# The second MLP's first 256 rows, summed on TensorE from x2 and the last expert's kept tiles

## The chip, the cores and the metric

The kernel runs on one core of a Trainium2 chip. The metric is the device time of one execution in microseconds, the median of several runs; lower is better. The profile's engines are PE (TensorE matmul), PEld (TensorE weight load), DVE (VectorE), ACT (ScalarE), POOL (GpSimd) and SP (SyncE, which here issues most of the DMAs).

## The reference

Three stages follow each other. An attention with gates and a running state gives 3072 tokens of 320 features. A mixture of 8 experts sends each token to the one expert that its gate logits choose; the expert's row is scaled by a gate weight and lands in the token's row of the result. A second MLP of width 2048 runs over all 3072 rows. Cut to what matters here:

```python
x = attn_out.transpose(0, 2, 1, 3).reshape(B * S, H * D)     # 3072 x 320
e_idx = np.argmax(x @ w_gate, axis=1)
out = np.zeros((N, D))
for e in range(8):
    mask = e_idx == e
    h = np.maximum(x[mask] @ w1[e], 0.0)                      # 320 -> 1024
    out[mask] = gate_w[mask, None] * eom[mask, e, None] * (h @ w2[e])
h = out @ w_in                                                # 320 -> 2048
return np.maximum(0.01 * h, h) @ w_out
```

## The kernel before, in words

Attention sorts the tokens on the fly into slots by expert. In the expert loop, each expert takes 3 or 4 tiles of 112 or 128 tokens: GpSimd gathers the tokens by indirect DMA, TensorE computes the first half for all of them (`ph`) and then, tile by tile, the second half (`po`, 24 matmuls a tile). ScalarE reads each `po` tile out of PSUM with the token's gate as scale (`yo`), and GpSimd scatters the rows by indirect DMA to their places in the DRAM tensor `x2` (`put`, printed in the profile as `x<-yo,ms`). The last expert has 3 tiles of 112 tokens. Between two scatters GpSimd writes a one-element `gap`; the scatters are declared independent of each other.

While an expert runs, the weights of the next but one are loaded and split into a high and a low part (`w1h`, `w1l`, `w2h`, `w2l`). In the last expert these are the second MLP's weights, loaded by SP as `r<-wf_in` and `r<-wf_out`.

Experts that got more tokens than their tiles hold are served by a loop of `overflow_tile` (`tc.For_i`, line 1351). With these inputs it makes no trip, but each engine goes through its branch. Then the second MLP runs over `GROUPS` of rows: 256, then five groups of 512, then 256. A group's rows are loaded from `x2` (`x2r`), turned so that features lie on partitions (`pxm` by TensorE for the first group, `xtm` by VectorE for the others), and split (`xhm`, `xlm`); 16 blocks `p` of 8 matmuls each follow, whose results ScalarE, VectorE and GpSimd turn into `lk`, `g2h` and `g2l`; then the second half (`po`) and the store.

Around the change these lines set the order; the two `keep_warm` calls are matmuls whose result nobody reads (12 ahead of the loop, 7 behind it):

```python
keep_warm(nc, psum, wts[E].w1h[:, 0], WARM[1])
...
    with tc.For_i(0, more, 1) as r:
...
xrs = {0: rows(0)}
ctx.enter_context(tc.manual_schedule(engines=ORDERED))
keep_warm(nc, psum, wts[E].w1h[:, 0], WARM[2])
for f in range(4):
    wts[E + 1].split2(f, V)
x = Tokens(nc, ap, psum, ident, xrs.pop(0), "m0").all()
```

Under `manual_schedule` the four compute engines keep the order in which the code is written. Outside of it (from the end of the expert block to the second `manual_schedule`) a scheduler may move instructions; in the order before, three of the four `w2h` casts and one `w2l` of `split2` stand ahead of the loop. A DMA waits on semaphores on the engine that issues it. DMAs take eight semaphore lanes in turn, `DMAHW0` to `DMAHW7` for those of SP and ScalarE, `DMASW0` to `DMASW7` for GpSimd's.

Of the kernel before, what the change touches and what calls it, by code (L numbers as in the profile page):

```python
# [10 lines left out]
F32 = mybir.dt.float32  # L11
# [5 lines left out]
ALU = mybir.AluOpType  # L17
# [500 lines left out]
class Router:  # L518
# [51 lines left out]
        nc.gpsimd.iota(self.meta, pattern=[[P, NC_], [S, B], [0, 4]], base=0, channel_multiplier=1)  # L570
        self.order.setup()

    def clear(self):

        put = self.nc.sync.dma_start
        late = lambda b: self.xd[b * S + (NC_ - 2) * P : (b + 1) * S].rearrange("(t p) e -> p t e", p=P)
        return [lambda: put(self.slots.rearrange("(p r) w -> p r w", p=P), self.init)] + [
            lambda b=b: put(late(b), self.zero[:, None, :].to_broadcast([P, 2, DM])) for b in range(B)
        ]

    def sink(self, c, b):
        if b == 0:
# [343 lines left out]
class Tokens:  # L926
# [8 lines left out]
    def dup(self):  # L935
        self.nc.vector.tensor_copy(self.xr[:, :, DM:DW], self.xr[:, :, 2 * P : DM])
# [72 lines left out]
class Expert:  # L1009
# [39 lines left out]
    def out(self, w, gs, ms, j, tag):  # L1049
        self.put(self.rows(w, gs, ms, j, tag), ms, j)  # L1050

    def rows(self, w, gs, ms, j, tag):
# [3 lines left out]
        mm2(self.nc, po, gs, ws, j)  # L1056
        return self.scaled(po, ms, j, tag)

    def scaled(self, po, ms, j, tag):
        yo = (self.ypool or self.pool).tile([P, DM], F32, tag="yo", name=f"yo{tag}_{j}", bufs=2 if self.ypool else 3)  # L1060
        yo = yo[: ms.shape[0]]
        self.nc.scalar.activation(yo, po, AF.Copy, scale=ms[:, j, 2:3].bitcast(F32))
        return yo

    def put(self, yo, ms, j):
        if self.puts is not None:
            self.nc.gpsimd.memset(self.gap, 0)
        put = self.nc.gpsimd.indirect_dma_start(
            out=self.x2,
            out_offset=bass.IndirectOffsetOnAxis(ap=ms[:, j, 1:2], axis=0),  # L1070
            in_=yo,
            in_offset=None,
            bounds_check=NT - 1,
            oob_is_err=False,
        )
        if self.puts is not None:
            apart(self.tc, put, self.puts, "every token is in one slot")


class Fill:  # L1080
# [65 lines left out]
def mlstm_moe_mlp(  # L1146
# [37 lines left out]
    def slots_of(e):  # L1184
        return ms[: ROWS[e], e, 0 if e else NJ // 2 : TILES[e]]
# [12 lines left out]
    with ExitStack() as actx:  # L1198
        h0 = actx.enter_context(tc.tile_pool(name="h0pool", bufs=1))
        exh = Expert(nc, h0, psum, ident, xd, x2, True, cpool)  # L1200
        exh.tc, exh.puts, exh.gap = tc, [], cpool.tile([1, 1], I32, name="gap2")
        msa = ms[:, 0, 0 : NJ // 2]
        fill = Fill(exh, msa, wts[0])

        def bumped():
            load_slots(0, 0, NJ // 2, P)

        router = Router(tc, actx, psum, ident, w_gate, w_og, slots, xd, stage, order, bumped)
        half = {}
# [12 lines left out]
        parts = w.steps([V, V, G, V, V, V, G])  # L1222
        todo = []

        def clear():
            todo.extend(router.clear())
# [10 lines left out]
        feed.update({i: [nxt] for i in (4, 5, 6, 7, 8, 9, 12, 13, 14, 15)})  # L1237
# [5 lines left out]
    wslot.append(ctx.enter_context(tc.tile_pool(name="wslot1", bufs=1)))  # L1243
    with ExitStack() as mctx:
        mp = mctx.enter_context(tc.tile_pool(name="mpool", bufs=2))
        cv = mctx.enter_context(tc.tile_pool(name="cvpool", bufs=1))
# [18 lines left out]
        for e in range(E):  # L1265
# [72 lines left out]
            if tk:  # L1338
                tk.turn()
                xs = tk.split()  # L1340
                tk = ex.x(ex.gather(slots_of(e + 2), e + 2), e + 2) if e + 2 < E else None
            for j in range(nj):
                ex.out(wts[e], gs, m, j, e)
                for act in late[j]:
                    act()

    keep_warm(nc, psum, wts[E].w1h[:, 0], WARM[1])
    with ExitStack() as octx:
        op = octx.enter_context(tc.tile_pool(name="opool", bufs=1))
        ex = Expert(nc, op, psum, ident, xd, x2, True)  # L1350
        with tc.For_i(0, more, 1) as r:
            e = nc.values_load(order.owner[0:1, ds(r, 1)], engines=SP, min_val=0, max_val=E - 1)
            row = nc.values_load(order.rows[0:1, ds(r, 1)], engines=SP, min_val=0, max_val=E * REG - P)
            overflow_tile(nc, op, ex, slots, w1, w2, e, row)

    ap = ctx.enter_context(tc.tile_pool(name="ap", bufs=2))
    gp = ctx.enter_context(tc.tile_pool(name="gp", bufs=1))
    GROUPS = [(0, HCAP)] + [(r, CAP) for r in range(HCAP, NT - CAP, CAP)] + [(NT - HCAP, HCAP)]

    def rows(i):  # L1360
        r, n = GROUPS[i]
        t = ap.tile([P, NJ * DM], F32, tag="x2r", name=f"x2r{i}", bufs=1)
        w = DM if i else DW
        t = t[:, : n // P * w].rearrange("p (j w) -> p j w", w=w)
        for j in range(n // P):
            nc.sync.dma_start(t[:, j, 0:DM], x2[r + j * P : r + (j + 1) * P])
        return t

    xrs = {0: rows(0)}
    ctx.enter_context(tc.manual_schedule(engines=ORDERED))  # L1370
    keep_warm(nc, psum, wts[E].w1h[:, 0], WARM[2])
    for f in range(4):
        wts[E + 1].split2(f, V)
    x = Tokens(nc, ap, psum, ident, xrs.pop(0), "m0").all()
    ws = [(wts[E + f // 8].w2h[:, f % 8], wts[E + f // 8].w2l[:, f % 8]) for f in range(F2 // P)]
    for i, (r, n) in enumerate(GROUPS):
        nxt, turns = None, []
        if i + 1 < len(GROUPS):
            nxt = Tokens(nc, ap, psum, ident, rows(i + 1), f"m{i + 1}")
            turns = nxt.pieces()  # L1380
        gs, lks = [], []

        def parts():
# [87 lines left out]
```

## Time and profile before

| | |
|---|---|
| median of 3 runs | 755.69 us (753.97 to 757.65) |
| the profiled execution | 753.32 us, its span 751.6 us |
| TensorE busy | 716.1 us, 95% of the span |
| VectorE, ScalarE, GpSimd busy | 449.8, 356.3, 350.2 us |
| mean granted TensorE clock | 0.979 of full |

Times in the rows are microseconds from the span's start. L1351 is line 1351 of the kernel before. A row of a timeline has start, duration, engine, line, operation, output from inputs, the shape and the count of instructions merged in it; in brackets stands the idle time ahead of it and what ended it. A row of the table by stages has the stage, its length, then for PE, PEld, DVE, ACT and POOL the busy time and the number of instructions, then the granted clock, the mean busy share of the 16 DMA engines and the GB/s. `SPq` and `PEldq` are the instruction queues (sequencers) of SP and TensorE, which carry semaphore waits, branches and the issue of DMAs.

### The profile page before, as it was taken

What the parts mean: (1) busy time and instruction counts of PE and PEld (TensorE: products, weight loads), DVE (VectorE), ACT (ScalarE), POOL (GpSimd) and SP (SyncE); (2) the same over time, 40 slices, a digit from 0 to 9 for tenths busy, and PEclk for the clock granted to TensorE, in tenths of its full rate; (3) what the DMA queues carried; (4) which work ended last, traced back from release to release, by engine and by line L of the source; (5) the groups of instructions that cost most, each with busy time, mean ns of one, the idle gap of its engine ahead of it and who ended that gap; (6) DMA issues with size and microseconds to landing.
All of it is one profiled execution on the core that took longest, in us unless ns stands there. A gap on an engine that the chain in (4) does not pass through costs nothing. (4 is left out here: it accounts for less than half of the span.)

```text
span 751.6 us, 14585 instructions
## 1 busy us (share of the span) xinstructions
PE 716.1 (95%) x5450; PEld 667.9 (89%) x5450; DVE 449.8 (60%) x936; ACT 356.3 (47%) x803; POOL 350.2 (47%) x396
## 2 busy tenths in 40 slices
PE   8798998899799999999998999999999999999998
PEld 6798987888689899999997989988988988988998
DVE  8988889674556758797765757048048048037020
ACT  5678677532463644663455355055045045046041
POOL 8758688655235474635123355046046046037041
PEclk9998999999799999999999999999999999999999
DMA  5887787411877677756662011001001000000000
GB/s 170 240 245 201 212 214 193 106 55 29 292 232 239 231 274 224 260 202 215 180 201 61 11 44 37 27 9 36 27 10 36 28 10 18 27 10 0 27 11 17
DMA packets 61743, 87.51 MB, mean 116 GB/s; under 512 B 8318, under 2 KB 53385, under 8 KB 60392
## 3 DMA queue, kind: packets, MB, share of 16 engines
q1 hardware_dynamic: 55880, 67.43, 30.0%
q10 hardware_dynamic: 2336, 10.75, 4.2%
q0 software_dynamic: 3456, 8.39, 3.5%
q8 instruction: 43, 0.70, 0.4%
q14 instruction: 28, 0.23, 0.1%
HBM read 67.69 MB, written 19.33 MB: 116 GB/s over the span
## 5 line engine op out<-in xcount | busy, mean ns | idle before, releaser
L1388 POOL TENSOR_TENSOR g2l<-lk,g2h 128x512 fp32r<-128x512 f32 (+1 forms) x112 | 126.6, 1133 | 214.0 <-ACT g2h L1387 203.7
L1397 DVE TENSOR_TENSOR lk<-p,lk 128x512 f32<-128x512 f32 (+1 forms) x112 | 68.9, 615 | 181.0 <-ACT lk L1396 179.1
L995 PE MATMUL p<-xhm,w1h 128*128 128x512 f32 (+1 forms) x336 | 119.6, 360 | 0.0
L995 PE MATMUL p<-xhm,w1l 128*128 128x512 f32 (+1 forms) x336 | 119.2, 359 | 0.0
L1006 PE MATMUL po<-w2h,g2l 128*128 128x320 f32 x384 | 118.7, 309 | 0.0
L1005 PE MATMUL po<-w2l,g2h 128*128 128x320 f32 x384 | 118.7, 309 | 0.0
L1004 PE MATMUL po<-w2h,g2h 128*128 128x320 f32 x384 | 118.6, 309 | 0.0
L1396 ACT ACTIVATE lk<-p 128x512 f32<-128x512 f32 (+1 forms) x112 | 60.1, 536 | 73.6 <-PE p L995 73.6
L995 PE MATMUL p<-xlm,w1h 128*128 128x512 f32 (+1 forms) x224 | 80.6, 360 | 0.0
L1004 PEld LDWEIGHTS po<-w2h,g2h 128*128 128x128 f32 x384 | 72.1, 188 | 0.2
L1005 PEld LDWEIGHTS po<-w2l,g2h 128*128 128x128 f32 x384 | 72.1, 188 | 0.2
L1411 ACT COPY yo<-po 128x320 f32<-128x320 f32 x24 | 10.2, 426 | 130.7 <-PE po L1006 130.7
L1006 PEld LDWEIGHTS po<-w2h,g2l 128*128 128x128 f32 x384 | 72.1, 188 | 0.0
L995 PEld LDWEIGHTS p<-xhm,w1l 128*128 128x128 f32 x336 | 63.5, 189 | 9.4
L995 PEld LDWEIGHTS p<-xhm,w1h 128*128 128x128 f32 x336 | 63.6, 189 | 9.4 <-DVE xhm L975 0.2
L1004 PE MATMUL po<-w2h,gh 128*128 128x320 f32 (+1 forms) x208 | 65.7, 316 | 0.0
L1005 PE MATMUL po<-w2l,gh 128*128 128x320 f32 (+1 forms) x208 | 65.0, 312 | 0.0
L1006 PE MATMUL po<-w2h,gl 128*128 128x320 f32 (+1 forms) x208 | 64.9, 312 | 0.0
L1387 ACT CAST g2h<-lk 128x512 fp32r<-128x512 f32 (+1 forms) x112 | 61.6, 550 | 1.6 <-DVE lk L1397 1.6
L957 DVE STREAM_TRANSPOSE xtm<-x2r 32x384 f32<-32x384 f32 (+3 forms) x144 | 59.6, 414 | 2.8
L995 PE MATMUL ph<-xh,w1h 128*128 128x384 f32 (+3 forms) x168 | 59.4, 354 | 0.0
L995 PE MATMUL ph<-xh,w1l 128*128 128x384 f32 (+3 forms) x168 | 59.3, 353 | 0.0
(252 smaller groups left out, 1547.9 us busy)
## 6 DMA issues: line engine op xcount, KB each, us to landing
r<-in_moe_w_dram SPq DMA_DIRECT2D x6, 1280.0 KB
r<-in_moe_w_dram SPq DMA_DIRECT2D x7, 1024.0 KB
raw<-in_moe_w_out_dram ACTq DMA_DIRECT2D x5, 1024.0 KB
r<-in_moe_w_dram SPq DMA_DIRECT2D x16, 256.0 KB
raw<-in_moe_w_in_dram ACTq DMA_DIRECT2D x4, 1024.0 KB
v<-in_v_dram SPq DMA_DIRECT2D x24, 164.0 KB
o<-in_o_gate_dram SPq DMA_DIRECT2D x6, 640.0 KB
k<-in_k_dram SPq DMA_DIRECT2D x24, 160.0 KB
```

What stands on the lines that cost most here:

```text
L957: self.nc.vector.transpose(out=xt[f, k].rearrange("p k (j t) -> p k j t", t=P)[:, :, :, t], in_=blocks[t, :, g].rearrange("p j k f -> p k ...
L995: nc.tensor.matmul(ps, a, b, start=(i == 0), stop=(i == len(seq) - 1))
L1004: nc.tensor.matmul(ps, gh[:, js], wh, start=(f == 0), stop=False)
L1005: nc.tensor.matmul(ps, gh[:, js], wl, start=False, stop=False)
L1006: nc.tensor.matmul(ps, gl[:, js], wh, start=False, stop=(f == n - 1))
L1387: nc.scalar.copy(gh, lk)
L1388: nc.gpsimd.tensor_sub(gl, lk, gh.bitcast(F32))
L1396: nc.scalar.activation(lk, pf, AF.Copy, scale=0.01)
L1397: nc.vector.tensor_max(lk, pf, lk)
L1411: nc.scalar.copy(yo, po[:, :DM])
```

## The change

A new class `Head` holds what the first 256 rows of the second MLP (`HCAP`) need, ahead of the loop.

- While the last expert runs, GpSimd writes the numbers 0 to 255 into `head_ids`; VectorE copies the token numbers of the expert's last two tiles and compares them, which gives two placing matrices `head_at` (112 x 256, a 1 where the slot's token is the row).
- Behind the first tile's scatter SP loads `x2[0:256]` into `head_x`. The last two tiles are read from PSUM into tiles of their own (`head_y`, `head_last`) and also scattered to `x2` as before.
- Behind the loop TensorE adds up, in PSUM and already turned, `head_x` (as plain matmuls against the identity) and the two kept tiles (each against its placing matrix). This takes the place of loading 256 rows from `x2` and transposing them.
- As `head_x` is read before the last two tiles are scattered, these 256 rows of `x2` are now cleared by a DMA of zeros in attention.
- The warm-up matmuls ahead of the loop go from 12 to 2, the 7 behind it go. The second `manual_schedule` begins right behind the loop, so all of `split2` stays behind it, and behind the split of the first rows. The next group's four loads are issued ahead of that split.

```diff
-WARM = (11, 12, 7)
+WARM = (11, 2)
...
-    def clear(self):
+    def clear(self, head):
...
+        ] + [lambda: put(head, self.zero[:, None, :].to_broadcast([P, 2, DM]))]
...
+    def keep(self, po, ms, j, yo, last):
+        g = ms[:, j, 2:3].bitcast(F32)
+        n = DM - 2 * P
+        self.nc.scalar.activation(yo, po, AF.Copy, scale=g)
+        both = po[:, None, 2 * P : DM].to_broadcast([po.shape[0], 2, n])
+        self.nc.scalar.activation(last.rearrange("p (c f) -> p c f", f=n), both, AF.Copy, scale=g)
...
+class Head:
...
+    def places(self, ms):
+        v, self.r = self.nc.vector, ms.shape[0]
+        v.tensor_copy(self.tok[: self.r], ms[:, 1:3, 1])
+        for j in range(2):
+            v.tensor_scalar(self.at[: self.r, j], self.ids[: self.r], self.tok[: self.r, j : j + 1], None, ALU.is_equal)
+
+    def load(self):
+        for j in range(HCAP // P):
+            self.nc.sync.dma_start(self.xr[:, j, 0:DM], self.x2[j * P : (j + 1) * P])
...
+    def turn(self, psum):
+        pts, mm, r = [], self.nc.tensor.matmul, self.r
+        for kt in range(3):
+            f = slice(kt * P, (kt + 1) * P)
+            pt = psum.tile([P, 512], F32, tag="ps", name=f"pxm0_{kt}")[:, :HCAP]
+            mm(pt, self.part(0, kt), self.at[:r, 0], start=True, stop=False)
+            for h in range(HCAP // P):
+                mm(pt[:, h * P : (h + 1) * P], self.xr[:, h, f], self.ident, start=False, stop=False)
+            pts.append(pt)
+        for kt, pt in enumerate(pts):
+            mm(pt, self.part(1, kt), self.at[:r, 1], start=False, stop=True)
+        return pts
...
+            if e == E - 1:
+                head.number(cv)
+                head.places(m)
             for j in range(nj):
-                ex.out(wts[e], gs, m, j, e)
+                if e == E - 1 and j:
+                    yo = head.yo[j - 1][: m.shape[0]]
+                    ex.rows(wts[e], gs, m, j, e, (yo, head.last[: m.shape[0], j - 1]))
+                    ex.put(yo, m, j)
+                else:
+                    ex.out(wts[e], gs, m, j, e)
+                    if e == E - 1:
+                        head.load()
...
+    ctx.enter_context(tc.manual_schedule(engines=ORDERED))
+    head.dup()
+    pts = head.turn(psum)
+    hctx.close()
...
-    xrs = {0: rows(0)}
-    ctx.enter_context(tc.manual_schedule(engines=ORDERED))
-    keep_warm(nc, psum, wts[E].w1h[:, 0], WARM[2])
+    nxt = Tokens(nc, ap, psum, ident, rows(1), "m1")
+    x = Tokens(nc, ap, psum, ident, head.xr, "m0")
+    x.pts = pts
+    x = x.split()
     for f in range(4):
         wts[E + 1].split2(f, V)
-    x = Tokens(nc, ap, psum, ident, xrs.pop(0), "m0").all()
```

GpSimd, the last expert's three scatters to `x2` (printed `x_79`), before. In brackets stands what the instruction waits for; a scatter waits for the earlier use of its own lane, so these three are on DMASW5, 6 and 7, and `L1351` is the loop's branch:

```order
L1068 DMA x_79<-yo_0_5408,ms 3072x320 [waits DMASW5_49,Activation_49]
L1067 MEMSET gap_91 1x1 [waits Pool_49]
L1068 DMA x_79<-yo_1_5443,ms 3072x320 [waits DMASW6_49,Activation_49]
L1067 MEMSET gap_91 1x1 [waits Pool_49]
L1068 DMA x_79<-yo_2_5476,ms 3072x320 [waits DMASW7_49,Activation_49]
L1351 COMPARE_AND_BRANCH
```

The same place in the changed kernel, where lines carry later numbers:

```order
L1106 IOTA head_ids 128x256
L1079 MEMSET gap_91 1x1 [waits Pool_49]
L1080 DMA x_79<-yo_0_5423,ms 3072x320 [waits DMASW5_49,Activation_49]
L1079 MEMSET gap_91 1x1 [waits Pool_49]
L1080 DMA x_79<-head_y_5392,ms 3072x320 [waits DMAHW3_49,DMAHW4_49,DMASW6_49,Activation_49]
L1079 MEMSET gap_91 1x1 [waits Pool_49]
L1080 DMA x_79<-head_y_5393,ms 3072x320 [waits DMASW7_49,Activation_49]
L1429 COMPARE_AND_BRANCH
```

The second scatter has gained two waits, for the lanes DMAHW3 and DMAHW4, and an `iota` stands ahead of the first.

SP in the changed kernel, from the last weights' loads to the loop's branch. ScalarE's casts wait for lanes 7, 0 and 1 for the three loads from `wf_in`, so the load from `wf_out` has lane 2 and the two of the head lanes 3 and 4:

```order
L803 DMA r_5326<-wf_in 128x2x1024 [waits DMAHW3_49,DMAHW2_49,DMAHW4_49,DVE_49,Activation_49]
L804 DMA r_5326<-wf_in 64x1024
L805 DMA r_5326<-wf_in 64x1024 [waits DMAHW1_49]
L811 DMA r_5389<-wf_out 128x8x320 [waits DMAHW5_49,DMAHW6_49,DVE_49,Activation_49]
L1119 DMA head_x<-x_79 128x320 [waits DMASW5_49]
L1119 DMA head_x<-x_79 128x320
L1429 COMPARE_AND_BRANCH
```

The two rows of `L1119` are new at this place, and they wait for the first scatter's lane, DMASW5. Before, the branch followed the `wf_out` load, and the first rows' loads stood behind the loop.

TensorE behind the loop, in the changed kernel; before, 7 `warm` matmuls and 6 transposes of 128 columns stood here:

```order
L1137 MATMUL pxm_0_5624<-head_at,head_y_5392 128x256
L1139 MATMUL pxm_0_5624<-ident,head_x 128x128 x2
L1137 MATMUL pxm_1_5628<-head_at,head_y_5392 128x256
L1139 MATMUL pxm_1_5628<-ident,head_x 128x128 x2
L1137 MATMUL pxm_2_5632<-head_at,head_last 128x256
L1139 MATMUL pxm_2_5632<-ident,head_x 128x128 [waits DVE_49]
L1139 MATMUL pxm_2_5632<-ident,head_x 128x128
L1142 MATMUL pxm_0_5624<-head_at,head_y_5393 128x256
L1142 MATMUL pxm_1_5628<-head_at,head_y_5393 128x256
L1142 MATMUL pxm_2_5632<-head_at,head_last 128x256
L997 MATMUL p_0_0_5670<-xhm_5651,w1h 128x256 [waits Activation_49]
```

The first `p` now follows 12 matmuls on fp32 tiles, 6 of 256 and 6 of 128 columns.

## Rows read from the trace of the kernel before

**Rows 1.** The page, part 1: busy us, share of the span, instructions.

```profile
PE 716.1 (95%) x5450; PEld 667.9 (89%) x5450; DVE 449.8 (60%) x936; ACT 356.3 (47%) x803; POOL 350.2 (47%) x396
```

**Rows 2.** The table by stages, three stretches around the seam.

```profile
383.30:393.90 10.60, 10.60 (x74) 10.60 (x73) 5.89 (x8) 3.54 (x6) 2.05 (x4) 1.00 1.00 281
393.90:398.90 5.00, 2.93 (x15) 2.09 (x13) 1.96 (x2) 3.34 (x5) 0.94 (x1) 1.00 0.17 52
399.60:403.00 3.40, 3.40 (x13) 2.54 (x11) 2.65 (x6) 1.01 (x4) 0.00 (x0) 0.50 0.24 74
```

**Rows 3.** The chain in order of time: start, duration, what.

```profile
401.68 1.28 PE pxm L944 x6
402.96 15.86 PE p L995 x128
```

**Rows 4.** SP's waits in 389:395, 394.91:396.3, 396.3:397.6: total us, times, longest.

```profile
SPq L1351 <- DMA x<-yo,ms: 5.6, 1, 5.6
...
SPq L1351 <- DMA x<-yo,ms: 6.9, 2, 5.6
...
SPq L1351 <- DMA x<-yo,ms: 1.2, 1, 1.2
```

**Rows 5.** Line 1351, TensorE's queue: count, ns min/median/max, first and last start.

```profile
L1351 PEldq EVENT_SEMAPHORE  x13: 51/51/51, 396.9 to 398.5; - x13
```

**Rows 6.** The timeline of PE behind the loop.

```profile
398.89 2.79 PE L67 MATMUL warm<-w1h 128*128 128x512 f32 x7 [2.07 <-issue]
...
402.61 0.54 PE L995 MATMUL p<-xhm,w1h 128*128 128x256 f32 x1
```

**Rows 7.** The timeline of POOL, the last expert's scatters.

```profile
387.88 0.98 POOL L1068 DMA_INDIRECT x<-yo,ms  x1 [9.92 <-ACT yo L1062]
...
391.44 0.96 POOL L1068 DMA_INDIRECT x<-yo,ms  x1 [2.53 <-ACT yo L1062]
...
394.96 0.94 POOL L1068 DMA_INDIRECT x<-yo,ms  x1 [2.50 <-ACT yo L1062]
```

**Rows 8.** The timeline of SP behind the loop.

```profile
398.28 6.46 SPq L1366 DMA_DIRECT2D x2r<-x  x6
```

**Rows 9.** The timeline of DVE in the seam.

```profile
390.26 1.22 DVE L910 TENSOR_TENSOR w1l<-r,w1h 128x1024 fp32r<-128x1024 f32 x1 [3.52 <-ACT w1h L893]
...
396.80 0.82 DVE L910 TENSOR_TENSOR w2l<-r,w2h 128x640 fp32r<-128x640 f32 x1
...
401.57 0.23 DVE L936 COPY x2r<-x2r 128x128 f32<-128x128 f32 x1
```

**Rows 10.** The timeline of POOL, two scatters of the first expert.

```profile
186.20 1.04 POOL L1068 DMA_INDIRECT x<-yo0a,ms  x1 [0.18 <-issue]
...
187.54 0.99 POOL L1068 DMA_INDIRECT x<-yo0a,ms  x1 [0.23 <-issue]
```

**Rows 11.** The timeline of PE in attention, fp32 matmuls of 128 columns.

```profile
99.71 1.28 PE L318 MATMUL psc<-qTm,kTm 128*128 128x128 f32 x10
```

**Rows 12.** The timeline of ACT ahead of the loop's branch.

```profile
395.52 1.97 ACT L901 CAST w2h<-r 128x640 fp32r<-128x640 f32 x3
```

**Rows 13.** Groups of ACT by form, 402 to 419: busy us, mean ns, idle before.

```profile
L1396 ACT ACTIVATE lk<-p 128x256 f32<-128x256 f32 x16 | 6.1, 384 | 5.7 <-PE p L995 5.7
L1387 ACT CAST g2h<-lk 128x256 fp32r<-128x256 f32 x14 | 5.6, 398 | 0.0
```

**Rows 14.** Groups of POOL by form, 402 to 419.

```profile
L1388 POOL TENSOR_TENSOR g2l<-lk,g2h 128x256 fp32r<-128x256 f32 x14 | 10.3, 737 | 13.2 <-DMA x2r<-x 10.3 <-ACT g2h L1387 3.0
```

**Rows 15.** The timeline of DVE at the end of the first group.

```profile
419.33 0.42 DVE L1397 TENSOR_TENSOR lk<-p,lk 128x256 f32<-128x256 f32 x1 [0.54 <-ACT lk L1396]
...
431.83 0.69 DVE L975 TENSOR_TENSOR xhm<-xtm,xhm 64x512 fp32r<-64x512 f32 x1
```

**Rows 16.** The timeline of PE, the second group's seventh matmul.

```profile
434.12 0.39 PE L995 MATMUL p<-xhm,w1h 128*128 128x512 f32 x1
```

**Rows 17.** Line 578, SP's writes of zeros: ns min/median/max, first and last start.

```profile
L578 SPq DMA_DIRECT2D xd<-zero x4: 377/378/2041, 87.9 to 109.1; - x4
```

More of the change, by code (lines that the diff above doesn't have):

```diff
@@ L571, in setup @@
         self.order.setup()
-    def clear(self):
+    def clear(self, head):
         put = self.nc.sync.dma_start
+        head = head.rearrange("(t p) e -> p t e", p=P)
         late = lambda b: self.xd[b * S + (NC_ - 2) * P : (b + 1) * S].rearrange("(t p) e -> p t e", p=P)
@@ L1050, in out, with rows @@
         self.put(self.rows(w, gs, ms, j, tag), ms, j)
-    def rows(self, w, gs, ms, j, tag):
+    def rows(self, w, gs, ms, j, tag, keep=None):
         ws = [(w.w2h[:, f], w.w2l[:, f]) for f in range(FE // P)]
@@ L1056, in rows @@
         mm2(self.nc, po, gs, ws, j)
+        if keep is not None:
+            return self.keep(po, ms, j, *keep)
         return self.scaled(po, ms, j, tag)
@@ L1077, in put, with __init__, number, again @@
             apart(self.tc, put, self.puts, "every token is in one slot")
+class Head:
+    def __init__(self, nc, pool, cp, x2, ident):
+        self.nc, self.x2, self.ident = nc, x2, ident
+        self.xr = pool.tile([P, HCAP // P, DW], F32, name="head_x")
+        self.at = pool.tile([P, 2, HCAP], F32, name="head_at")
+        self.last = pool.tile([P, 2, P], F32, name="head_last")
+        self.tok = pool.tile([P, 2], F32, name="head_tok")
+        self.cp = cp
+    def number(self, pool):
+        self.ids = pool.tile([P, HCAP], F32, tag="p", name="head_ids")
+        self.yo = [self.cp.tile([P, DM], F32, tag="yo", name=f"head_y{j}", bufs=2) for j in range(2)]
+        self.nc.gpsimd.iota(
+            self.ids, pattern=[[1, HCAP]], base=0, channel_multiplier=0, allow_small_or_imprecise_dtypes=True
+        )
+    def places(self, ms):
[6 more added lines that the diff above has]
+            self.nc.sync.dma_start(self.xr[:, j, 0:DM], self.x2[j * P : (j + 1) * P])
+    def again(self):
+        self.load()
+        self.nc.vector.memset(self.at, 0.0)
+    def dup(self):
+        self.nc.vector.tensor_copy(self.xr[:, :, DM:DW], self.xr[:, :, 2 * P : DM])
+    def part(self, j, kt):
+        return self.yo[j][: self.r, kt * P : (kt + 1) * P] if kt < 2 else self.last[: self.r, j]
+    def turn(self, psum):
[10 more added lines that the diff above has]
+        return pts
 class Fill:
@@ L1236, in mlstm_moe_mlp @@
         feed = {2: [clear], 3: [begin], 10: [load]}
-        feed.update({i: [nxt] for i in (4, 5, 6, 7, 8, 9, 12, 13, 14, 15)})
+        feed.update({i: [nxt] for i in (4, 5, 6, 7, 8, 9, 12, 13, 14, 15, 16)})
         side += [nop] * 6 + parts
@@ L1243, in mlstm_moe_mlp @@
     wslot.append(ctx.enter_context(tc.tile_pool(name="wslot1", bufs=1)))
+    hctx = ExitStack()
+    head = Head(nc, hctx.enter_context(tc.tile_pool(name="headpool", bufs=1)), cpool, x2, ident)
     with ExitStack() as mctx:
@@ L1354, in mlstm_moe_mlp @@
             overflow_tile(nc, op, ex, slots, w1, w2, e, row)
+            head.again()
+    ctx.enter_context(tc.manual_schedule(engines=ORDERED))
+    head.dup()
+    pts = head.turn(psum)
+    hctx.close()
     ap = ctx.enter_context(tc.tile_pool(name="ap", bufs=2))
@@ L1367, in rows @@
         return t
[L1369 to L1371 removed]
+    nxt = Tokens(nc, ap, psum, ident, rows(1), "m1")
+    x = Tokens(nc, ap, psum, ident, head.xr, "m0")
+    x.pts = pts
+    x = x.split()
     for f in range(4):
         wts[E + 1].split2(f, V)
[L1374 removed]
     ws = [(wts[E + f // 8].w2h[:, f % 8], wts[E + f // 8].w2l[:, f % 8]) for f in range(F2 // P)]
     for i, (r, n) in enumerate(GROUPS):
[L1377 to L1380, printed above, removed]
+        if i:
+            nxt = Tokens(nc, ap, psum, ident, rows(i + 1), f"m{i + 1}") if i + 1 < len(GROUPS) else None
+        turns = nxt.pieces() if nxt else []
         gs, lks = [], []
```

6 lines of the change are left out of this document (2 added, 4 removed).

## The prediction

> **What bounds the kernel now.** The page first: TensorE is busy for 95% of the span [rows 1], so a change can only pay where TensorE pauses or does filler work. The table by stages shows where that is. Up to 393.9 us TensorE runs the last expert without a gap, its clock at 1.00; from 393.9 to 398.9 it works 2.93 of 5.0 us, nearly all of it warm-up matmuls, and from 399.6 to 403.0 its clock stands at 0.50, the lower of its two levels (1.2 and 2.4 GHz) [rows 2]. This seam, between the last expert and the second MLP, is what the change rewrites; behind it the chain shows the first-half matmuls `p` of the first 256 rows in one piece, 128 in 15.86 us [rows 3].
>
> What ends last in the seam? Each engine runs through the branch of the `For_i` loop (no trip here) and waits there for every DMA still under way. SP's waits at line 1351 name the scatters `x<-yo,ms`: one of 5.6 us, then 1.3 (6.9 less 5.6), then 1.2 [rows 4]. The first ends between 394.91 and 395.0 (it lies whole in a window that closes at 395, and still counts in the one that opens at 394.91), so the three scatters land at about 394.9, 396.2 and 397.5. TensorE's sequencer goes through its 13 semaphore steps at this branch from 396.9 to 398.5 [rows 5], and its next matmul starts at 398.89 [rows 6]. So TensorE may go on 1.4 us after the third scatter has landed.
>
> **The change part by part.** The loop and its waits stay. What moves is when the last two scatters start.
>
> *The scatters.* The head's rows of x2 are loaded right after the first tile's scatter: the loads read x2, so they wait for that scatter; the two later scatters write x2, so they wait for both loads (the rows of GpSimd and SP above). Before, the three started at 387.88, 391.44 and 394.96 [rows 7], each as soon as its tile was scaled. Now:
> - first scatter landed: 394.9, as before. It takes 7 us while the DMA engines are full (share 1.00 from 383.3 to 393.9 [rows 2], the loads of the last weights); nothing in the change alters that.
> - both head loads landed: two loads of this size were issued from 398.28 on [rows 8], and VectorE's copy that needs both started at 401.57 [rows 9]: 3.3 us. So 398.2.
> - second scatter: 0.2 us for GpSimd's sequencer, 398.4. The third follows at the distance of two scatters that nothing holds up, 187.54 less 186.20 = 1.34 [rows 10]: 399.7 against 394.96, 4.8 us later.
> - third scatter landed: as before 2.5 us after its start (394.96 to 397.5), 402.2. TensorE goes on 1.4 later, at 403.6 instead of 398.89.
>
> Term: **+4.8 us**. Loads as quick as a scatter (2.5, and 0.4 for issuing the second) would give 4.4. A third scatter as slow as the second was (396.2 less 391.44, 4.8 us) would give 7.1; that one ran on full queues, and behind 393.9 the DMA share is 0.17 [rows 2], so I stay near 2.5, allow 1 us for a late packet, an estimate, and put the upper end at 5.8.
>
> The Trainium skill prices such a DMA (DMA: Bandwidth & Descriptors, section Anatomy of one DMA) at about 2.0 us plus its bytes by 436 GB/s: 2.3 us, an estimate, for 112 rows of 1280 bytes. The third scatter's 2.5 us agree within 0.2; the two loads would by that price take 2.4 and the second's issue of 0.4, and the term would be 4.3.
>
> *TensorE behind the branch.* Before: 7 warm-up matmuls and 6 transposes, 402.61 less 398.89 = 3.7 us to the first `p` [rows 6]. Now: 12 plain fp32 matmuls, 6 of 256 columns and 6 of 128. No row shows the 256-column form. The nearest is the 128-column fp32 `psc`, ten in 1.28 us at full clock [rows 11], so 0.13 apart; twice that for 256 columns. Full clock: 6 x 0.26 + 6 x 0.13 = 2.3 us. At the lower level the six 128-column transposes came 1.28/6 = 0.21 apart [rows 3], so 6 x 0.43 + 6 x 0.21 = 3.9 us. I take the lower level: TensorE will have stood idle from about 394.5 (two warm-up matmuls behind 393.9) to 403.6, while before a pause of 2.07 us [rows 6] was enough for 3.4 us at 0.50. Then the first `p` comes 3.9 us after the branch: term **+0.2** (at full clock -1.4).
>
> Before, the clock was back 4.1 us after TensorE's restart (403.0 less 398.89). The same delay ends here just behind the new matmuls, so I add nothing for a low clock under `p`. Should it last 2.7 us longer, half of that, 1.4 us, is lost.
>
> *Edits at nothing.* The 10 and 7 warm-up matmuls taken out filled a wait. ScalarE's three early `w2h` casts (1.97 us [rows 12]) and VectorE's one early `w2l` (0.82 [rows 9]) now stand behind the token split, so both have about 3 us of weight work (four each) when the first `p` is done, and `lk` starts that late. TensorE makes a `p` tile each 0.99 us (15.86/16); ScalarE needs 0.38 + 0.40, GpSimd 0.74, VectorE 0.42 for it [rows 13 to 15], so they win back 0.2 each time, 3 us in 15. If they don't, VectorE's transposes for the next group start late; those and the split ended at 432.5 (431.83 + 0.69 [rows 15]), and TensorE needed the result in its seventh matmul, at 434.12 [rows 16]: 1.6 us of cover. The four loads of the next rows wait for the new matmuls (the tile's space is reused): issued by 404.74 before (398.28 + 6.46 [rows 8]), now some 5 us later and landed by 413; VectorE takes them up behind its last `lk` of 419.33 [rows 15]. The `iota` fits into GpSimd's 9.92 us of idle time before the first scatter [rows 7], the cast and the two placing compares into VectorE's 3.52 before 390.26 [rows 9]. The two extra ScalarE copies (128 columns, so under `lk`'s 0.38 each) put off its last `w1h` cast, and all engines wait until 402.2 anyway. The zero write is a fifth DMA like four that took SP 0.38 to issue [rows 17], in a stage that TensorE's own work fills; uncovered, 0.4 us, at worst the 2.0 of the longest.
>
> **Sum:** 4.8 + 0.2 = +5.0 us. The profiled execution took 753.32, so 758.3. It lies 2.4 under the median of the runs, 755.69; against that the forecast is **760.7 us**.
>
> **Rivals.**
> - *The first scatter lands early* (not slower). Were it not behind the weight loads, it would land 2.5 us after 387.88, at 390.4, the head loads by 393.7, and the second scatter would start at 393.9, the third at 395.2, 0.25 late. TensorE goes on at 399.1, needs 2.3 to 3.9 us to the first `p` and so stands at -1.2 to +0.4: 754.5 to 756.1. All hangs on that landing: from 391 on it puts off the third scatter one for one. For it: with a free queue a scatter needs 2.5 us. Against it: the 5.6 us wait of [rows 4], in the very same place. The Trainium skill (same page, section Queues, rings and completion order) says that a DMA engine takes turns between the queue rows that it has work for, packet by packet, which would give this case; the trace of before does not agree, 7 us for this scatter.
> - *The branch holds nothing back* (faster; the last landings are not waited for, and the reload is saved). TensorE would go on 2.0 us behind its two warm-up matmuls, at 396.5, and reach the first `p` at 398.8 to 400.4, so -3.8 to -2.2: 751.9 to 753.5. Against it: the three waits of [rows 4] and the steps of [rows 5], which the change leaves in the program.
> - *Clock and lag on top*: the low clock lasts into the `p` matmuls (+1.4), ScalarE and VectorE are not level again within their cover (+0.5), or a packet is late (+1): 762 to 764.5. For it: 9 us without a matmul are four times the pause of before. Against it: the clock came back within 4.1 us here.
>
> **How the numbers follow.** Forecast 0.70, early landing 0.15, branch without hold 0.07, on top 0.08. The forecast's own range is +3.0 (4.4 less 1.4) to +6.5 (5.8, 0.2 and half a microsecond of lag): 758.7 to 762.2. The range 755.3 to 763.5 leaves out the branch case, half of the early landing and a third of the last, 0.17. The measurement of this kernel tells about 0.5% from no change, 3.8 us. Of the forecast I put 0.58 beyond that and 0.12 within: slower 0.58 + 0.08 = 0.66; same 0.12 + 0.15 + 0.02 (of the branch case) = 0.29; faster 0.05.
>
> **What would show it.** In the trace after: the head loads are issued near 395; the second scatter starts near 398.4 and the third near 399.7; TensorE is idle from about 394.5 to 403.6, behind two warm-up matmuls; the 12 new matmuls are 0.43 and 0.21 us apart; the first `p` is near 407.5. The forecast is wrong if the second scatter starts before 396, if TensorE restarts before 401, or if the new matmuls take over 4.5 us (the 256-column form dearer than two of 128).

## The result

The changed kernel takes 765.56 us (median of 6 runs, 760.89 to 766.25) against 757.56 for the kernel before on the same chip (6 runs, 753.97 to 758.57): ratio 1.0102, 95% interval 1.0077 to 1.0127, so 8.0 us or 1% slower. Forecast were +5.0 and 760.7 us; the direction held, the size did not. The 755.69 from which the forecast started was the median of the first three of these six runs, so +5.0 on 757.56 would be 762.6, and 3.0 us remain that the change itself cost beyond the forecast.

The profiled execution took 764.67 us (span 762.9). The page's first part, then the same three stretches as in [rows 2], moved to this run's seam (end of the last expert, wait, new matmuls; columns as there):

```profile
PE 719.4 (94%) x5451; PEld 673.0 (88%) x5451; DVE 452.3 (59%) x939; ACT 356.2 (47%) x805; POOL 350.1 (46%) x397
```

```profile
385.20:395.80 10.60, 10.60 (x75) 10.60 (x74) 6.59 (x11) 3.81 (x7) 1.02 (x2) 1.00 0.98 279
395.80:406.40 10.60, 0.60 (x4) 0.17 (x3) 1.45 (x2) 1.72 (x3) 1.96 (x3) 0.64 0.19 57
406.40:413.50 7.10, 7.10 (x24) 5.98 (x24) 0.00 (x0) 0.00 (x0) 0.00 (x0) 0.58 0.00 1
```

TensorE's busy time hardly changed (719.4 against 716.1), yet the span is 11.3 us longer. In the second stretch TensorE works 0.60 of 10.60 us; in the third, 24 matmul instructions, not 12, take 7.10 us at a granted clock of 0.58. The chain, in order of time (start, duration, what), says what the wait consists of:

```profile
389.78 6.46 DMA x<-yo,ms
396.25 0.34 SPq L1119
396.64 3.73 DMA head_x<-x
...
401.17 0.43 POOL x L1080
...
402.43 2.53 DMA x<-head_y,ms
...
406.17 0.24 DVE head_x L1127
406.40 1.20 PE pxm L1137 x2
407.61 0.85 PE pxm L1139 x4
408.46 0.85 PE pxm L1137 x2
...
411.88 1.65 PE pxm L1142 x6
413.55 0.38 ACT xhm L973
413.95 0.44 DVE xlm L975
414.43 15.68 PE p L997 x127
```

First scatter, head loads, second and third scatter (the timeline of GpSimd puts them at 401.17 and 402.43, against [rows 7]), landing, branch, new matmuls, split, `p`: each step starts when the one ahead of it is done. TensorE's queue goes through its 13 steps at the branch with the last one at 406.0 (398.5 in [rows 5]):

```profile
L1429 PEldq EVENT_SEMAPHORE  x13: 51/51/51, 396.4 to 406.0; - x13
```

**A measure that is steadier than the total.** Runs of one kernel spread over 4 to 8 us; in the profiles most of this lies ahead of the last expert's scatters. From the start of its first scatter to the end of the span, by contrast, the kernel before takes 751.6 less 387.88 = 363.7 us, and 363.6 in a second profile. After: 762.9 less 389.78 = 373.1, and 373.0 in a second one. So the seam costs 9.4 us. All kernels by this measure, in us from that start (third scatter, TensorE going on behind the branch, first `p` in its timeline, end of the span); the ratio is to the kernel before on the same chip. Each of the other kernels has one profile only, so a few tenths of a us in it may be chance:

| kernel | third scatter | TensorE on | first `p` | end | ratio (95%) |
|---|---|---|---|---|---|
| before | 7.1 | 11.0 | 14.7 | 363.7 | 1 |
| before, again | 7.1 | 11.0 | 14.7 | 363.6 | |
| after | 12.7 | 16.6 | 24.2 | 373.1 | 1.0102 (1.0077 to 1.0127) |
| after, again | 12.6 | 16.5 | 24.0 | 373.0 | 1.0090 (1.0066 to 1.0113) |
| e1 no wait | 7.0 | 11.9 | 18.3 | 367.2 | 1.0012 (0.9990 to 1.0034) |
| e2 before + wait | 11.6 | 15.5 | 19.8 | 368.8 | 1.0046 (1.0023 to 1.0068) |
| e3 before + zero write | 7.1 | 11.0 | 14.8 | 363.6 | 1.0014 (0.9989 to 1.0039) |
| e4 F32R placing | 13.1 | 17.1 | 21.7 | 372.1 | 1.0079 (1.0044 to 1.0114) |
| e5 42 warm-ups | 11.6 | 17.7 | 24.0 | 372.9 | 1.0086 (1.0054 to 1.0117) |
| e6 three kept | 7.0 | 13.9 | 13.9 | 362.3 | 0.9999 (0.9973 to 1.0024) |
| e8 three kept, F32R | 7.1 | 12.0 | 12.0 | 361.9 | 0.9973 (0.9955 to 0.9991) |
| e9 before, few warm-ups | 7.1 | 13.7 | 15.1 | 365.0 | 1.0024 (1.0000 to 1.0048) |

### The profile page after: what moved, and what is told of

Same layout as the page of the kernel before. It is cut to its first block, busy times and chain, and to the rows that moved or that the text cites. A ratio compares the mean times of both kernels' runs of the same rounds, so it can differ in the third digit from the quotient of the medians.

```text
span 762.9 us, 14594 instructions
## 1 busy us (share of the span) xinstructions
PE 719.4 (94%) x5451; PEld 673.0 (88%) x5451; DVE 452.3 (59%) x939; ACT 356.2 (47%) x805; POOL 350.1 (46%) x397
## 4 chain that ended last, share of the span: by engine, by line
PE 70%; DVE 10%; issue 8%; DMA 4%; POOL 4%; ACT 3%; SPq 0%; DVEq 0%; POOLq 0%; another core or an unknown queue 0%; ACTq 0%
PE p L997 23%; PE po L1008 9%; PE po L1006 9%; PE po L1007 9%; PE ph L997 6%; PE psc L319 3%; PE ppv L377 2%; PE pu L356 1%; ACT pe L289 1%; PE pin L340 1%; POOL x L1080 1%; DVE ww L326 1%; PE rt L595 1%; DMA x<-yo,ms 1%; DMA xr<-xd,ms 1%
```

## The experiments

### The two costs, one at a time

**e1**, the changed kernel with head loads that no scatter holds up:

```diff
-    head = Head(nc, hctx.enter_context(...), cpool, x2, ident)
+    head = Head(nc, hctx.enter_context(...), cpool, xd, ident)
```

> The changed kernel, but the head's 256 rows are loaded from xd instead of x2 (so the head rows hold other values), which no scatter writes: nothing holds the last two scatters back. Theory A (two costs in the seam: the scatters' wait for the head loads, about 5.6 us by the two traces, and the new matmuls behind the branch, 7.15 us where 3.9 were forecast, because each plain fp32 matmul is two instructions): the three scatters start 3.5 us apart again, TensorE goes on about 11 us behind the start of the first one, the turn still takes 7.15 us at the lower clock, and the time is some 3.5 us above the kernel before, 761. Rival B (all of the loss is the wait): 757 to 758, as before. Rival C (the zero write or something else ahead of the seam costs 1.9 us, as the later start of the first scatter in the profiled execution, 389.78 against 387.88, suggests): 762 to 763.

The scatters are 3.5 us apart again and TensorE goes on at 11.9, but the turn still takes 6 us. The chain:

```profile
398.57 3.45 DMA x<-head_y,ms
...
403.45 1.21 PE pxm L1137 x2
404.66 0.85 PE pxm L1139 x4
```

To the end 367.2, 3.5 above before. That is theory A's amount, in part by luck: 0.9 of it is the last scatter, which needed 3.45 us here instead of 2.5, and 2.7 the turn, whose clock came back after 3.7 us. The timed runs stand only 1.1 us above before, 759.05 against 757.93, with an interval of -0.8 to +2.6 us: under theory A's 761 and close above rival B's 758. They do not decide between the two; the trace does, by the turn in it ("What lies ahead of the seam", below, is on the difference between trace and timed runs).

**e2**, the kernel before with the zero write and the loads, but with its own turn:

```diff
                 ex.out(wts[e], gs, m, j, e)
+                if e == E - 1 and j == 0:
+                    for t in range(HCAP // P):
+                        nc.sync.dma_start(hx[:, t, 0:DM], x2[t * P : (t + 1) * P])
...
```

> The kernel before, with the zero write and the two head loads behind the last expert's first scatter, into a tile that nobody reads: the wait alone, with warm-ups, transposes and order as before. Theory A: second scatter about 10.4 us behind the end of the first one's start instead of 3.6, TensorE behind the branch some 5 to 5.6 us later, time 762.5 to 763.5. Rival B (all of the loss is the wait): 765 to 766. Rival C: 1.9 more than A, 764.5 to 765.5, with the first scatter near 389.8.

The chain:

```profile
388.80 6.58 DMA x<-yo,ms
395.40 0.34 SPq L1350
395.78 2.30 DMA head_x<-x
...
398.88 0.44 POOL x L1069
...
400.41 2.51 DMA x<-yo,ms
402.93 1.42 issue
404.34 3.35 PE warm L67 x7
```

TensorE goes on 4.5 us later than in the kernel before, and the end comes 5.1 later (368.8 less 363.7); timed 3.5 us (1.7 to 5.2 by the interval). This is the wait alone, and it is close to what the prediction's first term had (4.8). The wait is not all of the loss: rival B, which wanted 765 to 766, falls with 760.68. Theory A's 762.5 to 763.5 was too high as well.

One at a time the two costs are 4.5 us (restart, e2) and 2.7 us (turn, e1), 7.2 together. The 2.2 that are left to the 9.4 of the change stand in the traces too: its restart comes 1.1 later than in e2 (16.6 against 15.5), as its head loads were slower, and its turn takes 1.1 longer than in e1 (7.6 against 6.4 us to the first `p`), as its clock stayed low for 6.0 us instead of 3.7. In the timed runs the two single costs come by their ratios to 0.9 and 3.5 us, 4.4 together, against 8.0 and 6.8 for the change; so the account of the seam rests on the profiles.

**e3**, the zero write alone in the kernel before (the lines of `clear` and the `feed` entry 16 of the change):

> The kernel before with the fifth zero write alone. Theory A: no difference, 757 to 758, and the first of the last expert's scatters starts at 387 to 389 as in other executions of the kernel before. Rival C: 1.9 us more, 759.5, first scatter near 389.8.

757.85 against 757.93, and 363.6 to the end. Rival C is not borne out, though this run alone does not exclude it: the interval, -0.8 to +3.0 us, still holds the 1.9, and the first scatter started at 389.16, between the two forecasts. The second profiles speak against it: the first scatter of the kernel before started at 387.88 and 388.39, that of the changed kernel, zero write and all, at 389.78 and 387.34.

**e4**, the placing matmuls as F32R:

```diff
-        self.at = pool.tile([P, 2, HCAP], F32, name="head_at")
-        self.last = pool.tile([P, 2, P], F32, name="head_last")
+        self.at = pool.tile([P, 2, HCAP], F32R, name="head_at")
+        self.last = pool.tile([P, 2, P], F32R, name="head_last")
...
-        self.yo = [self.cp.tile([P, DM], F32, tag="yo", name=f"head_y{j}", bufs=2) for j in range(2)]
+        self.yo = [self.cp.tile([P, DM], F32R, tag="yo", name=f"head_y{j}", bufs=2) for j in range(2)]
...
```

> The changed kernel with the kept rows and the placing matrices as F32R (the low bits of the kept rows are left out), so that the six 256-column placing matmuls are one instruction each; the six 128-column ones with the identity stay plain fp32. Theory A: placing matmuls 0.25 us each at the lower clock instead of 0.85 (128 p matmuls of 256 columns take 15.7 us at the full clock, 0.12 each), so the turn shrinks from 7.15 to about 3.6 us, and the time from 765.6 to 762. Rival B (the matmuls' count does not matter, the wait is all): 765 to 766.

The chain, and a table by stages (length, then busy time of each engine, granted clock, DMA share, GB/s):

```profile
408.86 0.85 PE pxm L1139 x4
409.71 0.21 PE pxm L1137
409.92 0.85 PE pxm L1139 x4
```

```profile
408.30:412.90 4.60, 4.18 (x18) 3.89 (x18) 0.00 (x0) 0.38 (x2) 0.00 (x0) 0.50 0.01 2
412.90:417.00 4.10, 4.06 (x18) 3.89 (x19) 4.02 (x7) 3.32 (x7) 0.00 (x0) 0.50 0.56 164
417.00:430.40 13.40, 13.40 (x113) 13.40 (x113) 6.42 (x16) 9.55 (x28) 9.58 (x14) 1.00 0.00 0
```

The same table for the changed kernel, the first 6 us behind its restart:

```profile
406.40:412.40 6.00, 6.00 (x20) 5.37 (x21) 0.00 (x0) 0.00 (x0) 0.00 (x0) 0.50 0.00 1
```

One 256-column placing matmul now is one instruction of 0.21 us instead of two that take 0.85, and the first `p` comes some 4.7 us behind the restart instead of 7.6. But the clock stayed at 0.50 for 8.7 us behind the restart (408.3 to 417.0) instead of 6.0 (406.4 to 412.4 in the changed kernel), so the first 4.1 us of `p` ran at the lower clock. The turn became 2.9 us shorter; 0.4 went to a later restart and 1.4, half of what the turn gained, to the low clock under `p`. To the end 372.1 instead of 373.1: 1.0 us won of the 3.6 expected. The timed runs, 765.02, lie in rival B's range (765 to 766) and not at theory A's 762, and their interval (1.0044 to 1.0114) holds the changed kernel's ratio. So only the trace shows the price of the matmul's form: on plain fp32 tiles two instructions that take 0.85 us together, in F32R one of 0.21. What a shorter turn is worth depends on the clock behind it.

### The clock

**e5**: `WARM = (11, 42)` instead of `(11, 2)` in the changed kernel.

> The changed kernel with 42 warm-up matmuls ahead of the loop instead of 2, so that TensorE works at about 0.21 us each until some 2 us before it may go on. Theory A (the wait and the doubled fp32 matmuls at the lower clock): TensorE still goes on 16.6 us behind the first scatter's start, the first p follows 3.9 us earlier at the most (turn 3.6 us at the full clock instead of 7.15), the stretch from the first scatter to the end shrinks from 373.2 to 369.5 and the time from 765.6 to 762. Rival B (a pause of 2 us is enough to lose the clock, as in the kernel before): the turn takes 5 to 6 us, 763.5 to 764.5. Rival C (the clock has no part in it, the turn's length is its own): turn 7 us, time unchanged.

The timeline of PE (start, length of the group, line, operation; in brackets the idle time before):

```profile
397.33 9.70 PE L68 MATMUL warm<-w1h 128*128 128x512 f32 x42
409.03 0.70 PE L1137 MATMUL pxm<-head_at,head_y 112*128 112x256 f32 x2 [1.99 <-issue]
```

```profile
397.30:407.10 9.80, 9.74 (x44) 7.73 (x42) 1.22 (x1) 1.72 (x3) 1.96 (x3) 1.00 0.23 70
...
409.00:410.50 1.50, 1.47 (x9) 1.36 (x10) 0.00 (x0) 0.00 (x0) 0.00 (x0) 1.00 0.04 11
410.55:413.95 3.40, 3.40 (x14) 3.04 (x13) 0.00 (x0) 0.00 (x0) 0.00 (x0) 0.50 0.00 0
```

The clock was at 1.00 up to the pause, and the first placing matmuls ran at full speed; then it fell for 3.4 us, as after a like pause in the kernel before [rows 2, 6] (but not in every execution of it, see the end of "What lies ahead of the seam"). So the first `p` came 6.3 us behind the restart instead of 7.6. But 42 were too many: the last ended at 407.04 (409.03 less 1.99), and TensorE went on 1.99 us behind it, 1.1 us later than in the changed kernel. Net 0.2 us. Rival B comes nearest (764.32), and the trace shows a second condition at this branch: TensorE went on 1.4 us behind the last landing in the kernels above, but here, where that had passed, only 2 us behind its own last matmul. In the kernel before both fall on the same moment: 398.89 is 2.07 behind its warm-ups [rows 6] and 1.4 behind the landing.

**e9**: the kernel before with `WARM = (11, 2, 0)`: 2 warm-ups ahead of the loop, none behind it.

> The kernel before with the changed kernel's 2 warm-up matmuls ahead of the loop and none behind it, nothing else. Theory A (the restart waits for the third scatter's landing): TensorE goes on 11 us behind the first scatter as before, the 6 transposes take 1.3 us at the lower clock, the first p comes 12.5 to 13.2 behind the first scatter (14.7 before), p loses up to 1.7 us to the lower clock: from the first scatter to the end 362.5 to 364 (363.7 before), time as before. Rival (the restart waits for TensorE's own last matmul, so fewer warm-ups let it go on earlier): restart at 9 to 10, 2 us faster.

The chain, then the timeline of PE:

```profile
398.69 0.34 SPq L1366
...
399.08 2.23 DMA x2r<-x
```

```profile
401.31 1.72 PE L944 MATMUL pxm<-ident,x2r 128*128 128x128 f32 x6 [7.08 <-DMA x2r<-x]
```

Neither of the two. SP is through the branch at 398.7, 11.1 behind the first scatter (10.4 in the kernel before; the third scatter took 3.2 us to land here, 0.7 more than there), and issues the head's loads there; they land 2.6 us later, and TensorE, whose queue is through the branch at 399.0, has nothing else to do until then (13.7 instead of 11.0). In the kernel before the 7 warm-ups filled this stretch without putting anything off: in its second profile (c1, below) the reload landed at 402.27, 13.9 behind the first scatter, and the last transposes waited for it. Here the end comes 1.3 us later (365.0), the clock being low under the first 3.3 us of `p`. So the wait that the change removes, the reload of the head behind the branch, is real: 2.6 us here, 3.5 in c1 (issued at 398.78).

### A version that keeps the idea

**e6** loads the head's rows before the last expert (the scatters of the one before have landed by then), keeps all three tiles, and turns and splits ahead of the loop:

```diff
+            if e == E - 1:
+                head.rows_in(cv)
             gs = []
...
-                if e == E - 1 and j:
+                if e == E - 1:
...
+        head.room()
+        head.split(psum, True)
     keep_warm(nc, psum, wts[E].w1h[:, 0], WARM[1])
...
-            head.again()
+            head.again(op, psum)
...
-    x = Tokens(nc, ap, psum, ident, head.xr, "m0")
-    x.pts = pts
-    x = x.split()
+    x = (head.xh, head.xl)
```

> All three tiles of the last expert are kept and placed; the head's rows are loaded ahead of the last expert's first scatter, when the expert before has landed; the new matmuls and the split into high and low part stand ahead of the loop, and a trip of the loop (none here) would do them again from x2. Theory A: nothing holds the scatters back (3.5 us apart again), TensorE goes on at the branch 11 us behind the first scatter as in the kernel before, and the 15 fp32 matmuls (5.1 us at the full clock) are done in the wait, so that the first p comes 11 to 12.5 us behind the first scatter instead of 14.7 before and 24.2 after; from the first scatter to the end 361 to 362 against 363.7; time 755 to 756 against 757.7. Rival B (the head loads run into the weight loads and put these off, or the placing holds the last scatter up): first p later than 14.7, 758 or more. Rival C (what the change costs lies ahead of the seam): 759 or more with the first p at 11 to 12.5.

The timeline of PE:

```profile
394.58 1.03 PE L1137 MATMUL pxm<-head_box,head_y 112*128 112x256 f32 x4
395.45 0.61 PE L1141 MATMUL pxm<-ident,head_x 128*128 128x128 f32 x4
...
399.63 0.81 PE L68 MATMUL warm<-w1h 128*128 128x512 f32 x2
402.49 0.51 PE L997 MATMUL p<-head_xhl,w1h 128*128 128x256 f32 x2 [2.04 <-DVEq L1448]
```

The scatters are 3.5 us apart, and `p` follows the branch at once. But the 30 instructions and 2 warm-ups end at 400.44, 2.05 us ahead of the restart, and VectorE, with the split and a `w2l` cast, comes to the branch no earlier; its timeline:

```profile
401.12 0.83 DVE L912 TENSOR_TENSOR w2l<-r,w2h 128x640 fp32r<-128x640 f32 x1
```

Which of the two held the restart at 13.9, 2.9 us later than the scatters would have, this run does not tell apart. The restart is the first `p`: 13.9, not 11 to 12.5; to the end 362.3, 1.4 better than before, which the timed runs cannot see (0.9999).

**e8** shortens both: each kept tile as high and low part in F32R, so that a placing matmul is one instruction; no warm-ups behind it; the `w2h` and `w2l` casts spread over the first group:

```diff
+        for i, t in enumerate((self.hi[j], self.lo[j])):
+            self.nc.tensor.matmul(pt, t[: self.r, f], self.at[: self.r, j], start=start and not i, stop=stop and i == 1)
...
-    keep_warm(nc, psum, wts[E].w1h[:, 0], WARM[1])
...
+            if not i and f in (2, 4, 6, 8):
+                wts[E + 1].split2(f // 2 - 1, V)
```

> As the kernel with three kept tiles, but each kept tile as high and low part in F32R (24 placing matmuls more by count, but one instruction each, 18 of 0.12 us in place of 18 instructions of 0.22), without warm-ups behind the last tile, and with the w2h and w2l casts spread over the first group, so that they no longer stand ahead of the loop. Theory A (TensorE's restart at the loop is the later of the third scatter's landing plus 1.4 us and its own last matmul plus 2.05, and no engine may come to the loop later): matmuls done 9.5 to 10 us behind the first scatter, restart 11.5 to 12, first p directly, from the first scatter to the end 360 to 361 against 363.7 before and 362.4 with the fp32 form; time 754.5 to 755.5. Rival (ScalarE and VectorE come to the loop later than TensorE): first p at 13 to 14.5, no gain over the fp32 form.

The timeline of PE, then stages behind the last tile:

```profile
394.92 0.65 PE L1134 MATMUL pxm<-head_at,head_hl 112*128 112x256 f32 x4
...
398.29 0.28 PE L1134 MATMUL pxm<-head_at,head_lo 112*128 112x256 f32 x1
400.82 0.50 PE L997 MATMUL p<-head_xhl,w1h 128*128 128x256 f32 x2 [2.25 <-DVEq L1453]
```

```profile
394.90:400.80 5.90, 3.67 (x32) 3.47 (x30) 3.27 (x7) 3.01 (x7) 0.94 (x1) 1.00 0.17 56
400.80:405.00 4.20, 4.18 (x22) 4.18 (x23) 0.84 (x2) 1.06 (x3) 0.07 (x1) 0.59 0.55 157
```

Matmuls done 9.7 us behind the first scatter, restart at 12.0 (2.25 us behind the last matmul; VectorE's split ended at 400.23, so it came last), which is the first `p`, as expected; the end comes at 361.9 and not at 360 to 361. The clock fell for 3.4 us under `p` here (0.59 in the second stretch), while in e6 it stayed at 1.00 behind a pause of 2.04 us: `p` began 1.9 us earlier than there and the end came only 0.4 earlier. Timed 752.50 against 754.27 on this chip, ratio 0.9973 (0.9955 to 0.9991): about 2 us faster than the kernel before (0.7 to 3.4), and the one version whose interval lies under 1.

### What lies ahead of the seam

Both kernels once more, without an edit; first the kernel before, then the changed one:

> The kernel before, profiled once more. If what lies ahead of the last expert differs from run to run by itself, the first scatter of the last expert starts anywhere in 387 to 392 here too, and from it to the end 363.7 us pass again.

> The changed kernel once more, timed in more rounds. If its own cost lies all in the seam: from the first scatter to the end 373 us again, first scatter between 388 and 392, time 7 to 9.5 us above the kernel before.

Both seams repeat within 0.2 us (table above). The stretch ahead of them does not. The kernel before, first profile, then second: the timeline of PE at a pause in the expert two ahead of the last, and the table by stages there.

```profile
340.01 0.55 PE L944 MATMUL px<-ident,xr 128*128 128x128 f32 x3 [2.43 <-DVE xr L936]
```

```profile
339.00:343.00 4.00, 2.99 (x21) 3.00 (x22) 4.00 (x9) 0.48 (x1) 1.86 (x2) 1.00 0.75 266
```

```profile
338.98 0.55 PE L944 MATMUL px<-ident,xr 128*128 128x128 f32 x3 [2.44 <-DVE xr L936]
```

```profile
338.00:342.00 4.00, 3.02 (x16) 3.02 (x17) 4.00 (x8) 0.48 (x1) 1.89 (x2) 0.77 0.78 272
```

The same pause of 2.4 us, and once the clock stays at 1.00, once it falls; from here to the first scatter it is 47.87 us (387.88 less 340.01) and 49.41 (388.39 less 338.98). This 1.5 us appears in six of seven profiles of kernels without the change's head code (before, again; e2, e3, e6, e8, e9), and in none of the five with it (after, twice; e1, e4, e5). It could be a part of why the changed kernel's timed loss, 8.0 and 6.8 us (1.0090 of 754.27), lies 1.4 to 2.6 under the 9.4 of its seam, and e1's as far under its own. But the profiles do not bear it out as the whole: what lies further ahead differs too, and the first scatter started at 387.34 to 391.58 in the five profiles with this head code, at 387.56 to 389.16 in the seven others, so not earlier. That the 1.5 us go with the change is only a count of twelve profiles; what would cause it is not shown, and why the timed loss is smaller than the seam's stays open.

The same holds for the clock behind the loop. In the first profile of the kernel before it was at 0.50 for 3.4 us [rows 2]; in the second, behind a pause of 2.05 us at the same place, it did not fall:

```profile
399.40:404.00 4.60, 3.78 (x17) 2.51 (x18) 3.40 (x7) 1.65 (x4) 0.00 (x0) 1.00 0.26 75
```

The first `p` came 14.7 behind the first scatter in both, and the end 363.7 and 363.6: with the reload still to land, the low clock cost nothing there.

## Why the prediction was right in direction and wrong in size

- **What bounds the seam**: right. Third landing plus 1.4 us sets TensorE's restart, and with e5 there is a second condition that fell on the same moment in the trace of before and was not seen there.
- **The scatter term, +4.8 (4.4 to 5.8)**: mechanism right, size near. Measured: restart 16.6 instead of 11.0 behind the first scatter, +5.6 in the changed kernel, +4.5 in e2. Step by step in the changed kernel: the first scatter landed in 6.5 us (7.0 forecast); the loads took 4.1 from issue to landing (0.34 + 0.04 + 3.73; 3.3 forecast; 2.7 in e2); GpSimd 0.8 us from landing to scatter (0.2 forecast); third scatter 1.26 later, landed in 2.53, restart 1.4 later, all within 0.1 of the forecast. The 5.6 lie inside the range, as it happens, because errors of both signs met: without the last part of the second load, which came at 400.37 when the 15 others were there at 398.92, the loads would have taken 2.7 us as in e2. For such a late packet the range had allowed 1 us. The price that the prediction takes from the Trainium skill (DMA: Bandwidth & Descriptors, Anatomy of one DMA) is stated there for DMAs that GpSimd issues: the third scatter agrees (2.53 against an estimate of 2.3 by it), but the two loads are issued by SP, and what the prediction works out for them by that price has no ground in that section.
- **TensorE behind the branch, +0.2 (3.7 to 3.9 us)**: this is the step that failed. It measured 7.6 us from restart to first `p`, 3.9 more than before. The prediction priced a matmul of 128 columns by `psc`, "ten in 1.28 us" [rows 11], and took each of these rows for a matmul of the program. They are instructions, and a matmul on plain fp32 tiles is two of them: the program has 192 `psc` matmuls (24 units of 8 heads), the trace of before lists, at the `psc` line with its count and ns (min, median, max),

```profile
L318 PE MATMUL psc<-qTm,kTm x384: 275/275/528, 9.9 to 158.2; 128*128 128x128 f32 x192
```

  384. The transposes, which it had used for the lower clock, are one instruction each (`pxm` x6 in [rows 3]), so a 128-column fp32 matmul costs twice a transpose, not the same: 0.85/2 = 0.43 at the lower clock instead of 0.21, and 0.85 instead of 0.43 for 256 columns. With that the step reads 6 x 0.85 + 6 x 0.43 = 7.7 us at the lower clock; 7.15 came, its last 1.1 us at the full clock, and 0.4 for the split between the last of them and the first `p`, for which the prediction had no term. (Its own products, 6 x 0.43 + 6 x 0.21, add to 3.8, not 3.9.) The condition named in the prediction, over 4.5 us for the new matmuls, was met, but not for the reason named: 256 columns cost 0.85 us, just two of 128, and it is both forms that cost twice the forecast. The Trainium skill has the price (FP8 and Floating Point Precision, TensorE Precision Notes): true fp32 goes through the array in 4 passes. By it an estimate is four times the 0.21 us that the F32R form of 256 columns took at the lower clock in e4, taken as one pass: 0.84 us; the rows above agree with 0.85 us.
- **Clock**: the lower level for the turn was rightly taken. That it comes back 4.1 us behind the restart was one row's value; it was 6.0 in the changed kernel, 8.7 in e4, 3.7 in e1, and in the second profile of the kernel before the clock had not fallen at all. Under `p` nothing was lost in the changed kernel, since the turn was long enough to take all of it.
- **Edits at nothing**: for the zero write no run shows a cost (e3), and the casts that were moved hold: with four `w2h` casts behind the split, it is 16.1 us from the first `p` to the first `po` (430.11 less 413.97) against 16.2 (418.81 less 402.61 in [rows 6]), and the second group's seventh matmul comes 31.5 us behind the first `p` (445.42 less 413.97) against 31.5 (434.12 in [rows 16] less 402.61). The warm-ups taken out cost nothing behind the wait. In the kernel before they were not idle filler in every execution: with them the low clock lay under filler and transposes, without them (e9) under 3.3 us of `p`.
- **Rivals**: the first scatter did not land early (6.5 us), and the branch held everything back. "Clock and lag on top" came nearest (762 to 764.5; the 765.56 lie above it, and its own terms on top of 760.7 reach only 763.6), but not by its reasons: there was no lag and no clock lost under `p`; only the late packet came.
- **The sum**: 5.6 + 3.9 - 0.1 = 9.4 us in the seam against 5.0 forecast. Of the 4.4 between them, 3.7 are the step that failed and 0.8 the scatter term.

## What to carry to other kernels

Before costing a matmul from a trace, count the instructions that the program's matmul becomes: divide the trace's count at that line by the program's own, once for each data type and for transposes. A load that reads what a scatter has just written, and that the next scatter must wait for, strings together DMA latencies that had run side by side; load it a stage earlier or keep the data that is missing. Work that replaces a reload behind a barrier is best done in the wait ahead of the barrier: by the trace the same idea cost 9.4 us behind it and won 1.4 (e6) and 1.8 (e8) ahead of it, of which the timed runs show a gain for e8 alone.

## What the runs showed of the hardware that was not expected

- This loop without a trip cost TensorE 2.0 us between its last matmul and its next (1.99 in e5, where the last landing was past by about 3.5 us: third scatter at 402.97, plus the 2.53 of the changed kernel 405.5, restart 409.03); filler ahead of it would have to end that much earlier. e5 is the one run that shows this apart from the landing.
- The granted clock after a pause was not a fixed price: behind the restart it stayed low for 3.7 us (e1) to 8.7 us (e4). Behind the pauses of 5.3 to 10.5 us at this loop (after, twice; e1, e2, e4, e9) it was at 0.50 from the restart on; behind those of 2.0 to 2.3 us it fell within 1.5 us in the kernel before, e3, e5 and e8, and stayed at 1.00 in the second execution of the kernel before and in e6. After the 2.4 us pause further ahead it likewise fell in one execution of a program and not in another.
- Two equal head loads took 2.30 us from the start of the second one's issue in e2 and 3.73, 3.78 and 4.06 in three profiles of the changed head code (after, after again, e4). In each of these three, 15 of the 16 parts in which the second load lands were there and the last came 1.4 us or more behind them (after: 398.92 and 400.37; after again: 396.40 and 397.83; e4: 400.51 and 402.26); in e5, with the same head code, no part was late (the last two at 400.88 and 400.90). Why one part is late is open.
